# Prefetching DFT matrices, gating later loads and spreading row preparation in a fused S4 convolution and GLU MLP kernel

## The chip, the cores and the metric

The kernel runs on one core of a Trainium2 chip. The metric is the device time of one execution in microseconds (us), taken as the median of several runs; lower is better. The profiler's record of one execution has a *span*, which is about 2 us shorter than the device time of that execution (469.3 against 471.06 for the kernel before).

Engines are named as in the profile: PE is TensorE (matmuls), DVE is VectorE, ACT is ScalarE, POOL is GpSimd, and SP is SyncE, which here issues the DMA transfers. PEclk is the clock granted to TensorE, where 1.00 is full speed.

## The reference

The input `u` is [1, 2048, 640] in bf16. Cut to what matters:

```python
def _A_ref(u, A_re, A_im, B_re, B_im, C_re, C_im, log_dt, Dskip):
    ...                                             # K [640, 2048]: sums of complex exponentials
    Kf = rfft2(pad(K))[None]                        # zero-padded to 4096
    Uf = rfft2(pad(u.transpose(0, 2, 1)))
    y = irfft2(Uf * Kf)[..., :L]                    # long convolution by FFT
    return y.transpose(0, 2, 1) + u * Dskip

def _B_ref(x, w_gate, w_up, w_down):                # 640 -> 1728 -> 640
    return (sigmoid(x @ w_gate) * (x @ w_up)) @ w_down

x = A_u
h = x + _A_ref(_layernorm(x), ...)
h2 = h + _B_ref(_layernorm(h), ...)                 # the output
```

## The kernel before

The Fourier transforms are matmuls with constant DFT matrices. The 640 channels go in two halves of 320 columns (`HALVES`). After preparation (tables, first layer norm, spectrum of the input) three parts follow, and the change touches all three.

**1. Spectrum product, `kspec`.** There are 17 frequency groups q, taken in the order 16, 0, 1, ..., 15. Each needs a DFT matrix `mk` of 320 KB from DRAM. The pool `mkp` holds three of them.

```python
def front(qp):                                   # a pair of q
    W3 = mkp.tile(..., name="W3g");  sy.dma_start(W3..., cd["W3"]...)
    for qi, q in enumerate(qs):
        mk = mkp.tile([P, 2, 5, 128], BF16, name="mk")
        sy.dma_start(mk[:]..., cd["M"][q])                       # 320 KB
        ps = ps2.tile([P, 2, 512], F32, name="ps_xk", tag="p2")
        for ri in range(2):
            for j in range(5):                                   # 10 matmuls of 320 columns
                nc.tensor.matmul(ps[:, ri, 0:w], lhsT=mk[:, ri, j, :], rhs=kv[:, j, :], ...)
        nc.scalar.copy(xk[:, qi, :, :], ps[:, :, 0:w])
    ...                                          # DVE: products t1, t2 of xk with the input's spectrum xu
def back(qs, prods, W3):
    ...                                          # up to 8 matmuls into ps_g for each q
    nc.scalar.copy(stg[0][...], ps[:, :, 0:w])                   # g_stg
    if q % 2 == 1:
        sy.dma_start(d2[hf]..., stg[0][:])                       # to DRAM
```

**2. Hand-over.** The result `d2` comes back from DRAM as `g2` with rows on other partitions. For four tiles of 128 rows ("rows" below means such a tile), the skip term `us` and the last transform step are summed in PSUM, DVE adds the residual `h`, and layer norm and transposes follow. Only then can the first gate matmul run.

```python
def tail_loads(rc):                              # rc: row block of 4 tiles of 128 rows
    nc.sync.dma_start(h[:, 4*rc:4*rc+4, :], xv[:, 4*rc:4*rc+4, :])
    ...                                          # g2 of both halves, one DMA each
    return g2, [skip(h, 4*rc+i, sd) for i in range(4)]           # us: two DVE steps for each row

def prep(rc, loaded):
    is2(pso_p, "ml_po", rc, loaded)              # matmuls of us and g2, DVE: h += PSUM
    for r in range(r0, r0 + 4): ln_stats(st, mv, h, r)
    ln_coef(...)
    ...                                          # DVE: ln2 rows; PE: 20 transposes; DVE/ACT: copies to lnT
prep(0, first)
Wg, Wu, Wd = Wts()                               # 16 DMAs for gate, up, down weights
nxt = tail_loads(1)
```

**3. MLP.** Four row blocks of 512 rows. The hidden size 1728 makes 13 tiles of 128 and a tail of 64.

```python
FT = [(128 * i, 128) for i in range(13)] + [(1664, 64)]
for rc in range(4):
    for ft, (f0, fw) in enumerate(FT):
        for (ps, W) in ((pg, Wg), (pu, Wu)):
            for dc in range(5): nc.tensor.matmul(ps[0:fw, :], lhsT=W[:, dc, f0:f0+fw], rhs=lnT..., ...)  # 512 columns
        nc.scalar.activation(sg, pg, AF.Sigmoid);  nc.vector.tensor_tensor(hm, pu, sg, ALU.mult)
        if rc < 3 and ft == 4:
            prep(rc + 1, nxt)                    # the whole preparation of the next block, at once
            if rc < 2: nxt = tail_loads(rc + 2)
    ...                                          # down projection: 4 rows x 14 tiles x (512 + 128 columns)
```

## Time and profile before

The time before is 468.78 us (median of three runs, 464.31 to 470.15).

The span falls into stages whose limits differ. I cut it at the first `ps_xk` matmul of the second channel half, the end of its last `g_stg` copy, and the first gate or up matmul.

| stage of the kernel before | from – to, us | length, us | what limits it |
|---|---|---|---|
| preparation and first half | 0 – 179.6 | 179.6 | not changed |
| spectrum product, second half | 179.6 – 224.3 | 44.8 | waits for `mk` |
| hand-over | 224.3 – 248.1 | 23.7 | store, load of g2, sums, layer norm |
| MLP | 248.1 – 469.3 | 221.2 | TensorE |

These are the windows of the kernel before: the two middle stages, then the first two of the four row blocks. Columns: stretch and its length; then for each engine busy us (instructions); then granted clock, DMA busy share, GB/s.

```profile
core 0: us, PE busy (x) PEld busy (x) DVE busy (x) ACT busy (x) POOL busy (x), PEclk, DMA share, GB/s
179.60:224.30 44.70, 32.06 (x236) 19.21 (x236) 23.48 (x45) 21.64 (x33) 0.00 (x0) 0.96 0.92 295
224.30:248.10 23.80, 9.86 (x47) 5.39 (x48) 11.91 (x32) 1.21 (x3) 1.04 (x1) 0.58 0.97 338
248.10:305.60 57.50, 53.43 (x290) 26.18 (x293) 26.69 (x56) 10.81 (x17) 1.13 (x1) 0.94 0.09 30
305.60:363.00 57.40, 54.09 (x292) 26.56 (x296) 23.91 (x47) 9.53 (x16) 1.23 (x1) 0.94 0.03 12
```

In the first line TensorE works 32 of 44.7 us and the DMA engines are busy 92% of the time: this looks like a stage bound by bytes. In the second line the clock is 0.58. In the row blocks TensorE is busy nearly all the time, but each loses 3 to 4 us (the third, 56.0 us long, loses 2).

This is the chain of work that ended last in the kernel before, for the first two stages. Columns: start, duration, and what it was; "issue" is time in which the engine waited for nothing that the profile shows, and L446 is a line of the kernel (the numbers differ between kernels).

```profile
181.11 5.48 DMA mk<-s4c_M
186.59 0.04 issue
186.63 2.32 PE ps_xk L446 x10
...
224.36 3.10 DMA d_1_59<-g_stg
```

A `mk` line is a transfer from issue to landing; TensorE is idle in only a part of it. Three more such pieces stand in the chain, at 191.89, 204.32 and 214.67. After the last store the view goes on through Wd loads (down weights, not needed before the first down projection) and a g2 load of 8.20 us. That part misleads: `g_1_2622` in it is the g2 of the *second* block, which the first gate matmul doesn't need. The g2 load on which the hand-over hangs is `g_1_2468`, issued at 227.52 with Wd loads before and after it in the queue. The DMA view gives its time from issue to landing (size of one, then us):

```profile
g_1_2468<-d_1_59 SPq DMA_DIRECT2D x1, 640.0 KB, 6.2
```

This is what TensorE waits for in the kernel before, in the second half's stages and, after the dots, in the MLP. Columns: the waiting line and what it waited for; us in total, times, longest.

```profile
PE ps_xk L446 <- DMA mk<-s4c_M: 10.0, 5, 2.9
PE ps_y L505 <- DMA g_1_2468<-d_1_59: 7.4, 1, 7.4
...
PE ml_pt L641 <- DVE ln_2759 L637: 2.6, 1, 2.6
PE ml_pt L641 <- DVE ln_3191 L637: 2.2, 1, 2.2
```

Ten microseconds of waits for matrices are the largest single item. The transposes (`ml_pt`) in the MLP wait for DVE's layer-norm rows, because the whole preparation of a block is done in one bunch.

### The profile page before, as it was taken

The numbers are of one execution on the slowest core, as the hardware profiler recorded it, in microseconds if no ns is written. First come the engines' busy times: TensorE is split into PE (matmuls) and PEld (weight loads), VectorE is DVE, ScalarE is ACT, GpSimd is POOL, SyncE is SP. The second block draws the span as 40 slices with busy tenths as digits, with TensorE's granted clock in tenths as the row PEclk, the third lists the DMA queues.
The fourth block names the chain that finished last, engine by engine and source line by source line (L and its number), as shares of the span: only waits on it lengthen the run. The fifth ranks groups of instructions, "written<-read, shape, count | busy, mean of one in ns | idle before, by whom it ended". The sixth has DMA issues, their size and how long they took to land.

```text
span 469.3 us, 6215 instructions
## 1 busy us (share of the span) xinstructions
PE 353.4 (75%) x2412; PEld 188.2 (40%) x2435; DVE 276.6 (59%) x506; ACT 189.4 (40%) x323; POOL 9.9 (2%) x16
## 2 busy tenths in 40 slices
PE   1113643589997387876249799997999989999996
PEld 1001211276654174443125444544444444444443
DVE  4989899979999913554085843238322373322312
ACT  5989987466775363455003032020320203103210
POOL 0010100000000000000000000001000000000000
PEclk9999855569999679899569979999799999999999
DMA  8601654623997506799892300010000100010001
GB/s 242 243 1 56 219 202 128 181 68 87 284 303 246 162 1 239 242 315 299 287 377 94 113 0 1 0 57 1 1 0 1 56 1 0 1 55 2 0 16 42
DMA packets 47725, 54.23 MB, mean 116 GB/s; under 512 B 7056, under 2 KB 39888, under 8 KB 47696
## 3 DMA queue, kind: packets, MB, share of 16 engines
q1 hardware_dynamic: 47696, 53.84, 35.7%
q8 instruction: 19, 0.31, 0.3%
q14 instruction: 10, 0.08, 0.1%
HBM read 40.72 MB, written 13.11 MB: 115 GB/s over the span
## 4 chain that ended last, share of the span: by engine, by line
PE 38%; DVE 35%; issue 14%; DMA 9%; ACT 2%; POOL 1%; SPq 1%; POOLq 0%; DVEq 0%
PE ml_pg L656 10%; PE ml_po L670 9%; PE ml_pu L656 9%; DMA mk<-s4c_M 4%; PE pk L401 4%; DVE tabA L332 4%; DVE tS L330 4%; PE ps_xk L446 3%; DVE ln_st L250 3%; DVE tabB L347 2%; DVE tS L346 2%; DVE tabA L334 2%; DVE tabA L333 2%; DMA g_1_2622<-d_1_59 2%; PE ps_kv L412 1%
## 5 line engine op out<-in xcount | busy, mean ns | idle before, releaser
L659 DVE TENSOR_TENSOR ml_hm<-ml_pu,ml_sg 128x512 bf16<-128x512 f32 (+1 forms) x56 | 38.7, 691 | 79.2 <-PE ml_pu L656 69.8
L658 ACT ACTIVATE ml_sg<-ml_pg 128x512 bf16<-128x512 f32 (+1 forms) x56 | 33.4, 597 | 121.2 <-PE ml_pg L656 119.6
L656 PE MATMUL ml_pg<-lnT,Wg 128*128 128x512 bf16 (+1 forms) x272 | 71.1, 392 | 0.5 <-issue 0.2
L656 PE MATMUL ml_pu<-lnT,Wu 128*128 128x512 bf16 (+1 forms) x275 | 68.8, 379 | 0.3 <-issue 0.2
L670 PE MATMUL ml_po<-Wd,ml_hm 128*128 128x512 bf16 (+3 forms) x438 | 64.8, 298 | 0.6 <-issue 0.2
L446 PE MATMUL ps_xk<-kv,mk 128*128 128x320 bf16 x340 | 50.9, 303 | 14.1 <-DMA mk<-s4c_M 10.6
L670 PEld LDWEIGHTS <-ml_hm 128*128 128x128 bf16 x448 | 33.3, 98 | 31.8 <-issue 9.0
L446 PEld LDWEIGHTS <-mk 128*128 128x128 bf16 x340 | 32.8, 98 | 31.6 <-DMA mk<-s4c_M 13.7
L656 PEld LDWEIGHTS <-Wg 128*128 128x128 bf16 (+1 forms) x280 | 28.0, 102 | 35.3 <-issue 6.5
L656 PEld LDWEIGHTS <-Wu 128*128 128x128 bf16 (+1 forms) x280 | 27.6, 99 | 31.9
L672 DVE TENSOR_TENSOR ml_out<-ml_po,h 128x640 bf16<-128x640 f32 x16 | 13.2, 825 | 43.1 <-PE ml_po L670 43.1
L447 ACT CAST xk<-ps_xk 128x640 bf16<-128x640 f32 x34 | 23.5, 692 | 33.2 <-PE ps_xk L446 31.8
L642 ACT COPY lnT<-ml_pt 128x512 bf16<-128x512 bf16 x8 | 4.7, 586 | 62.6 <-PE ml_pt L641 62.6
L478 ACT CAST g_stg<-ps_g 128x640 bf16<-128x640 f32 x32 | 21.1, 697 | 8.8 <-PE ps_g L474 8.0
L361 PEld LDWEIGHTS <-c_F_102 128*128 128x128 bf16 x64 | 8.0, 125 | 41.1 <-issue 37.5
L401 PE MATMUL pk<-tabB,tabA 128*128 128x84 bf16 x320 | 19.2, 230 | 6.5 <-DVE tabA L333 4.6
L401 PEld LDWEIGHTS <-tabA 128*128 128x128 bf16 x320 | 17.0, 116 | 10.7 <-issue 10.0
L509 DVE TENSOR_TENSOR h<-ps_y,h 128x640 bf16<-128x640 f32 x16 | 12.8, 818 | 13.2 <-PE ps_y L505 12.0
L403 ACT CAST kts<-pk 128x420 bf16<-128x420 f32 x32 | 15.4, 511 | 12.1 <-PE pk L401 11.7
L332 DVE TENSOR_TENSOR tabA<-tabA 128x2240 bf16<-128x2240 bf16 (+2 forms) x16 | 18.9, 1194 | 0.0
L381 PEld LDWEIGHTS <-W2g 128*64 128x64 bf16 x136 | 8.3, 132 | 25.9 <-DMA W2g<-s4c_W 9.6
L330 DVE TENSOR_TENSOR tS<-tabA 128x2240 bf16<-128x2240 bf16 (+2 forms) x16 | 18.4, 1194 | 0.0
(335 smaller groups left out, 471.9 us busy)
## 6 DMA issues: line engine op xcount, KB each, us to landing
mk<-s4c_M SPq DMA_DIRECT2D x34, 320.0 KB, 4.5
d1u<-s_stg SPq DMA_DIRECT2D x16, 320.0 KB, 2.8
a2g<-d1u SPq DMA_DIRECT2D x16, 320.0 KB, 3.5
W3g<-s4c_W SPq DMA_DIRECT2D x16, 192.0 KB, 4.4
u<-in_A_u_dram SPq DMA_DIRECT2D x4, 640.0 KB, 6.3
d_0_58<-g_stg SPq DMA_DIRECT2D x8, 320.0 KB, 3.4
h<-in_A_u_dram SPq DMA_DIRECT2D x4, 640.0 KB, 8.4
d_1_59<-g_stg SPq DMA_DIRECT2D x8, 320.0 KB, 3.9
```

The source lines that it names most:

```text
L250: nc.vector.bn_stats(st[:, r, hh, :], src[:, r, 320 * hh:320 * hh + 320])
L330: V(t[:, ri], A[:, ri, :, s0:s1, :], bc(A[:, 1, :, b:b + 1, :], [P, G, n, 4]), ALU.mult)
L332: V(A[:, ri, :, d0:d1, :], A[:, ri, :, s0:s1, :], bc(A[:, 0, :, b:b + 1, :], [P, G, n, 4]), ALU.mult)
L401: nc.tensor.matmul(pk[:, i, :], lhsT=A[:, ri, g].rearrange("p e c -> p (e c)"), rhs=B[:, ri, :, 4 * g:4 * g + 4], start=(ri == 0), stop=(r ...
L403: nc.scalar.copy(kts[:, g0:g0 + 5, :], pk[:])
L446: nc.tensor.matmul(ps[:, ri, 0:w], lhsT=mk[:, ri, j, :], rhs=kv[:, j, :], start=(j == 0), stop=(j == 4))
L447: nc.scalar.copy(xk[:, qi, :, :], ps[:, :, 0:w])
L478: nc.scalar.copy(stg[0][:, 2 * (q % 2):2 * (q % 2) + 2, :], ps[:, :, 0:w])
L656: nc.tensor.matmul(ps[0:fw, :], lhsT=W[:, dc, f0:f0 + fw], rhs=rhs, start=(dc == 0), stop=(dc == 4))
L658: nc.scalar.activation(sg[0:fw, :], pg[0:fw, :], AF.Sigmoid)
L659: nc.vector.tensor_tensor(hm[0:fw, ft, :], pu[0:fw, :], sg[0:fw, :], ALU.mult)
L670: nc.tensor.matmul(po[:, c0:c0 + w], lhsT=hm[0:fw, ft, 128 * lr:128 * lr + 128], rhs=Wd[0:fw, ft, c0:c0 + w], start=(ft == 0), stop=(ft == ...
```

## The change

The change has five parts:

- eight DFT matrices of the second half are loaded early, into the slot of a tile (`xu0`) that is dead by then;
- Wd and the rows `h` of later blocks are *gated*: their loads wait for a small POOL copy from the first rows' layer-norm coefficients, so that they don't compete with the loads the hand-over needs;
- for the first four rows the residual is summed on TensorE with an identity matmul, and the layer-norm statistics are read from PSUM;
- the 64-wide tails of gate and up are merged into one 128-wide matmul;
- the preparation of the next row block is a generator, advanced one step for each tile from ft 5 on, with the transposes at ft 12.

The skip rows `us` also move, from the loads into the row sums. Three smaller edits go along: each g2 load is split into two of 320 KB, the first rows' layer-norm coefficients are computed by pairs of rows, and ACT computes two of the first four layer-norm rows.

```diff
+    NPRE = 8
+    def prefetch(kx):
+        mb = kx.tile([P, NPRE, 2, 5, 128], BF16, name="mk_pre", tag="X")       # xu0 has tag "X" too
+        for i in range(NPRE):
+            sy.dma_start(mb[:, i]..., cd["M"][QORD[i]])
 ...
-                mk = mkp.tile([P, 2, 5, 128], BF16, name="mk")
-                sy.dma_start(mk[:]..., cd["M"][q])
+                if pre is not None and QPOS[q] < NPRE:
+                    mk = pre[:, QPOS[q]]
+                else:
+                    ...                                                        # as before
 ...
+    def is2_row(rc, i, g2, h, us, psp, tag, stats=None):
 ...
+            if stats is not None:
+                nc.tensor.matmul(ps[:, hf, 0:w], lhsT=ident[:], rhs=h[:, r, o:o + w], start=False, stop=False)
 ...
+        else:
+            stats(r, ps[:, :, 0:w])                                            # bn_stats from PSUM
+            nc.scalar.copy(hv, ps[:, :, 0:w])
 ...
     drain(s2)
+    pre = prefetch(kx)
     kv = kmm(1, ktp, kx, dict(T))
 ...
+    def tail_loads(rc, gate=None):
+        if gate is not None:
+            nc.gpsimd.tensor_copy(h[:, rs, 0:1], bc(gate, [P, 4, 1]))
 ...
+def load_d(nc, wp, ins, gate):
     Wd = wp.tile([P, 14, 640], BF16, name="Wd", tag="B")
+    nc.gpsimd.tensor_copy(Wd[:, :, 0:1], bc(gate, [P, 14, 1]))
 ...
+            if rc < 3 and ft >= 5:
+                if ft == 5: pr = prep(rc + 1, nxt)
+                drain(pr, 1)
+                if ft == 8 and rc < 2: nxt = tail_loads(rc + 2, gate)
+                if ft == 12: turn(rc + 1)                                      # the transposes
 ...
+        for dc in range(5):                                                    # both 64-wide tails
+            nc.tensor.matmul(pg[:], lhsT=Wl[:, dc]..., rhs=rhs, ...)
```

More of the change, by code (lines that the diff above doesn't have):

```diff
@@ L428, in kmm, with kspec @@
         return kv
-    def kspec(hf, kv, xu, kw2, mkp, dve_add):
+    NPRE = 8
+    def prefetch(kx):
+        mb = kx.tile([P, NPRE, 2, 5, 128], BF16, name="mk_pre", tag="X")
+        for i in range(NPRE):
+            sy.dma_start(mb[:, i].rearrange("p a b c -> p (a b c)"), cd["M"][QORD[i]])
+        return mb
+    def kspec(hf, kv, xu, kw2, mkp, dve_add, pre=None):
         o, w = HALVES[hf]
@@ L440, in front @@
             for qi, q in enumerate(qs):
-                mk = mkp.tile([P, 2, 5, 128], BF16, name="mk")
-                sy.dma_start(mk[:].rearrange("p a b c -> p (a b c)"), cd["M"][q])
+                if pre is not None and QPOS[q] < NPRE:
+                    mk = pre[:, QPOS[q]]
+                else:
+                    mk = mkp.tile([P, 2, 5, 128], BF16, name="mk")
+                    sy.dma_start(mk[:].rearrange("p a b c -> p (a b c)"), cd["M"][q])
                 ps = ps2.tile([P, 2, 512], F32, name="ps_xk", tag="p2")
@@ L496, in skip @@
         return us
-    def is2(rc, g2, h, us4, psp, tag):
-        for i in range(4):
-            r = 4 * rc + i
-            ps = psp.tile([P, 2, 512], F32, name="ps_y", tag=tag)
-            for hf, (o, w) in enumerate(HALVES):
-                nc.tensor.matmul(ps[:, hf, 0:w], lhsT=ident[:], rhs=us4[i][:, o:o + w], start=True, stop=False)
-                for qp in range(2):
-                    nc.tensor.matmul(ps[:, hf, 0:w], lhsT=W4[:, qp, :], rhs=g2[hf][:, qp, i, :], start=False, stop=(qp == 1 and r < 12))
-                if r >= 12:
-                    nc.tensor.matmul(ps[:, hf, 0:w], lhsT=sel[0:4, r - 12, :], rhs=kl[0:4, o:o + w], start=False, stop=True)
-            hv = h[:, r, :].rearrange("p (a b) -> p a b", a=2)
+    def is2_row(rc, i, g2, h, us, psp, tag, stats=None):
+        r = 4 * rc + i
+        ps = psp.tile([P, 2, 512], F32, name="ps_y", tag=tag)
+        for hf, (o, w) in enumerate(HALVES):
+            nc.tensor.matmul(ps[:, hf, 0:w], lhsT=ident[:], rhs=us[:, o:o + w], start=True, stop=False)
+            if stats is not None:
+                nc.tensor.matmul(ps[:, hf, 0:w], lhsT=ident[:], rhs=h[:, r, o:o + w], start=False, stop=False)
+            for qp in range(2):
+                nc.tensor.matmul(ps[:, hf, 0:w], lhsT=W4[:, qp, :], rhs=g2[hf][:, qp, i, :], start=False, stop=(qp == 1 and r < 12))
+            if r >= 12:
+                nc.tensor.matmul(ps[:, hf, 0:w], lhsT=sel[0:4, r - 12, :], rhs=kl[0:4, o:o + w], start=False, stop=True)
+        hv = h[:, r, :].rearrange("p (a b) -> p a b", a=2)
+        if stats is None:
             nc.vector.tensor_tensor(hv, ps[:, :, 0:w], hv, ALU.add)
+        else:
+            stats(r, ps[:, :, 0:w])
+            nc.scalar.copy(hv, ps[:, :, 0:w])
     cb_product()
@@ L537, in full_kernel @@
     kx = sc.pool("xu", bufs=1)
-    xu0 = kx.tile([P, 17, 2, HALVES[0][1]], BF16, name="xu0")
+    xu0 = kx.tile([P, 17, 2, HALVES[0][1]], BF16, name="xu0", tag="X")
     ktp = sc.pool("kts", bufs=2)
@@ L572, in full_kernel @@
     dsk = tl.tile([P, D], BF16, name="dsk")
-    def tail_loads(rc):
-        nc.sync.dma_start(h[:, 4 * rc:4 * rc + 4, :], xv[:, 4 * rc:4 * rc + 4, :])
+    def tail_loads(rc, gate=None):
+        rs = slice(4 * rc, 4 * rc + 4)
+        if gate is not None:
+            nc.gpsimd.tensor_copy(h[:, rs, 0:1], bc(gate, [P, 4, 1]))
+        nc.sync.dma_start(h[:, rs, :], xv[:, rs, :])
         g2 = []
@@ L579, in tail_loads, with row @@
             v = d2[hf].rearrange("k (c a r) d -> (k c) a r d", c=4, a=2)
-            sy.dma_start(t[:], v[:, :, 4 * rc:4 * rc + 4, :])
+            for i in (0, 2):
+                sy.dma_start(t[:, :, i:i + 2, :], v[:, :, 4 * rc + i:4 * rc + i + 2, :])
             g2.append(t)
-        return g2, [skip(h, 4 * rc + i, sd) for i in range(4)]
-    drain(kspec(1, kv, xu1, kw2, mkp, True))
+        return g2
+    def row(psp, tag, rc, i, g2, stats=None):
+        r = 4 * rc + i
+        us = sd.tile([P, D], BF16, name="us")
+        nc.vector.tensor_scalar(us[:], h[:, r, :], rstd[:, r:r + 1], nmr[:, r:r + 1], ALU.mult, ALU.add)
+        nc.vector.tensor_tensor(us[:], us[:], dsk[:], ALU.mult)
+        is2_row(rc, i, g2, h, us, psp, tag, stats)
+    drain(kspec(1, kv, xu1, kw2, mkp, True, pre))
     sy.dma_start(dsk[:], ins["A_Dskip"].rearrange("(o d) -> o d", o=1).to_broadcast((P, D)))
@@ L587, in full_kernel @@
     sc.close("mk", "kw2", "a2", "kts", "xu", "ps_2", "ps_k")
-    mlp(nc, sc, h, lambda: load_gu(nc, wp, ins) + (load_d(nc, bp, ins),), ident, ov, ln_stats, ln_coef, first, tail_loads,
-        lambda psp, tag, rc, x: is2(rc, x[0], h, x[1], psp, tag))
+    mlp(nc, sc, h, lambda: load_gu(nc, wp, ins), lambda gate: load_d(nc, bp, ins, gate), ident, ov, ln_stats, ln_coef, first, tail_loads, row)
     sc.close("sd", "g2", "tl", "weights", "tabb", "consts", "dram")
+FT = 13
 def load_gu(nc, wp, ins):
-    Wg = wp.tile([P, 5, 1728], BF16, name="Wg")
-    Wu = wp.tile([P, 5, 1728], BF16, name="Wu")
+    Wg = wp.tile([P, 5, 1664], BF16, name="Wg")
+    Wu = wp.tile([P, 5, 1664], BF16, name="Wu")
+    Wl = wp.tile([P, 5, 2, 64], BF16, name="Wl")
     gv = ins["B_w_gate"].rearrange("(c p) f -> p c f", p=P)
     uv = ins["B_w_up"].rearrange("(c p) f -> p c f", p=P)
-    for f0 in range(0, 1728, 432):
-        nc.sync.dma_start(Wg[:, :, f0:f0 + 432], gv[:, :, f0:f0 + 432])
-        nc.sync.dma_start(Wu[:, :, f0:f0 + 432], uv[:, :, f0:f0 + 432])
-    return Wg, Wu
-def load_d(nc, wp, ins):
+    for f0 in range(0, 1664, 416):
+        nc.sync.dma_start(Wg[:, :, f0:f0 + 416], gv[:, :, f0:f0 + 416])
+        nc.sync.dma_start(Wu[:, :, f0:f0 + 416], uv[:, :, f0:f0 + 416])
+    nc.sync.dma_start(Wl[:, :, 0, :], gv[:, :, 1664:1728])
+    nc.sync.dma_start(Wl[:, :, 1, :], uv[:, :, 1664:1728])
+    return Wg, Wu, Wl
+def load_d(nc, wp, ins, gate):
     Wd = wp.tile([P, 14, 640], BF16, name="Wd", tag="B")
+    nc.gpsimd.tensor_copy(Wd[:, :, 0:1], bc(gate, [P, 14, 1]))
     for c in range(0, 13, 2):
@@ L608, in load_d, with mlp @@
         nc.sync.dma_start(Wd[:, c:c + n, :], ins["B_w_down"][128 * c:128 * (c + n), :].rearrange("(c p) f -> p c f", p=P))
-    nc.sync.dma_start(Wd[0:64, 13, :], ins["B_w_down"][1664:1728, :])
+    nc.sync.dma_start(Wd[64:128, 13, :], ins["B_w_down"][1664:1728, :])
     return Wd
-def mlp(nc, sc, h, Wts, ident, ov, ln_stats, ln_coef, first, tail_loads, is2):
+def mlp(nc, sc, h, gu, down, ident, ov, ln_stats, ln_coef, first, tail_loads, row):
     big = sc.pool("ml_big", bufs=1)
@@ L626, in mlp, with stats_first, turn @@
     nmr = big.tile([P, 16], F32, name="ln2_nmr")
+    def stats_first(r, src):
+        for hh in range(2):
+            nc.vector.bn_stats(st[:, r, hh, :], src[:, hh, :])
+        nc.vector.bn_aggr(mv[:, r, :], st[:, r, :, :].rearrange("p a b -> p (a b)"))
+        if r % 2:
+            ln_coef(mv, rstd, nmr, slice(r - 1, r + 1))
     def prep(rc, loaded):
         r0 = 4 * rc
-        is2(pso_p, "ml_po", rc, loaded)
-        for r in range(r0, r0 + 4):
-            ln_stats(st, mv, h, r)
-        ln_coef(mv, rstd, nmr, slice(r0, r0 + 4))
         ln2 = lnp.tile([P, 4, 640], BF16, name="ln2")
         for i in range(4):
-            r = r0 + i
-            nc.vector.tensor_scalar(ln2[:, i, :], h[:, r, :], rstd[:, r:r + 1], nmr[:, r:r + 1], ALU.mult, ALU.add)
+            row(pso_p, "ml_po", rc, i, loaded, stats_first if rc == 0 else None)
+            if rc:
+                ln_stats(st, mv, h, r0 + i)
+                yield
+        if rc:
+            ln_coef(mv, rstd, nmr, slice(r0, r0 + 4))
+        for i in range(4):
+            r = r0 + i
+            if rc == 0 and i % 2:
+                nc.scalar.activation(ln2[:, i, :], h[:, r, :], AF.Identity, scale=rstd[:, r:r + 1], bias=nmr[:, r:r + 1])
+            else:
+                nc.vector.tensor_scalar(ln2[:, i, :], h[:, r, :], rstd[:, r:r + 1], nmr[:, r:r + 1], ALU.mult, ALU.add)
+            if rc and i % 2:
+                yield
+        lns[rc] = ln2
+    lns = {}
+    def turn(rc):
+        ln2 = lns[rc]
         for dc in range(5):
@@ L641, in prep @@
                 nc.tensor.transpose(pt[:, i, :], ln2[:, i, 128 * dc:128 * dc + 128], ident[:])
-            (nc.scalar.copy if dc % 2 else nc.vector.tensor_copy)(lnT[:, dc, r0:r0 + 4, :], pt[:])
-    prep(0, first)
-    Wg, Wu, Wd = Wts()
-    nxt = tail_loads(1)
-    FT = [(128 * i, 128) for i in range(13)] + [(1664, 64)]
+            (nc.scalar.copy if dc % 2 else nc.vector.tensor_copy)(lnT[:, dc, 4 * rc:4 * rc + 4, :], pt[:])
+    drain(prep(0, first))
+    turn(0)
+    Wg, Wu, Wl = gu()
+    gate = nmr[:, 3:4]
@@ L648, in mlp, with up @@
+    Wd = down(gate)
+    nxt = tail_loads(1, gate)
     for rc in range(4):
+        pr = None
         hm = hmp.tile([P, 14, 512], BF16, name="ml_hm")
-        for ft, (f0, fw) in enumerate(FT):
+        def up(ps, W, f0):
+            for dc in range(5):
+                rhs = lnT[:, dc, 4 * rc:4 * rc + 4, :].rearrange("p a b -> p (a b)")
+                nc.tensor.matmul(ps[:], lhsT=W[:, dc, f0:f0 + 128], rhs=rhs, start=(dc == 0), stop=(dc == 4))
+        for ft in range(FT):
             pg = psg_p.tile([P, 512], F32, name="ml_pg", tag="ml_pg")
@@ L652, in mlp @@
             pu = psu_p.tile([P, 512], F32, name="ml_pu")
-            for (ps, W) in ((pg, Wg), (pu, Wu)):
-                for dc in range(5):
-                    rhs = lnT[:, dc, 4 * rc:4 * rc + 4, :].rearrange("p a b -> p (a b)")
-                    nc.tensor.matmul(ps[0:fw, :], lhsT=W[:, dc, f0:f0 + fw], rhs=rhs, start=(dc == 0), stop=(dc == 4))
+            up(pg, Wg, 128 * ft)
+            up(pu, Wu, 128 * ft)
             sg = tmp.tile([P, 512], BF16, name="ml_sg")
-            nc.scalar.activation(sg[0:fw, :], pg[0:fw, :], AF.Sigmoid)
@@ L659, in mlp @@
-            nc.vector.tensor_tensor(hm[0:fw, ft, :], pu[0:fw, :], sg[0:fw, :], ALU.mult)
-            if rc < 3 and ft == 4:
-                prep(rc + 1, nxt)
-                if rc < 2:
-                    nxt = tail_loads(rc + 2)
+            nc.scalar.activation(sg[:], pg[:], AF.Sigmoid)
+            nc.vector.tensor_tensor(hm[:, ft, :], pu[:], sg[:], ALU.mult)
+            if rc < 3 and ft >= 5:
+                if ft == 5:
+                    pr = prep(rc + 1, nxt)
+                drain(pr, 1)
+                if ft == 8 and rc < 2:
+                    nxt = tail_loads(rc + 2, gate)
+                if ft == 12:
+                    turn(rc + 1)
@@ new lines, in mlp @@
+        pg = psg_p.tile([P, 512], F32, name="ml_pg", tag="ml_pg")
+        for dc in range(5):
+            rhs = lnT[:, dc, 4 * rc:4 * rc + 4, :].rearrange("p a b -> p (a b)")
+            nc.tensor.matmul(pg[:], lhsT=Wl[:, dc].rearrange("p a b -> p (a b)"), rhs=rhs, start=(dc == 0), stop=(dc == 4))
+        sg = tmp.tile([P, 512], BF16, name="ml_sg")
+        nc.scalar.activation(sg[64:128, :], pg[0:64, :], AF.Sigmoid)
+        nc.vector.tensor_tensor(hm[64:128, FT, :], pg[64:128, :], sg[64:128, :], ALU.mult)
@@ L667, in mlp @@
             po = pso_p.tile([P, 640], F32, name="ml_po")
-            for ft, (f0, fw) in enumerate(FT):
+            for ft in range(14):
+                k0 = 64 if ft == FT else 0
                 for (c0, w) in ((0, 512), (512, 128)):
-                    nc.tensor.matmul(po[:, c0:c0 + w], lhsT=hm[0:fw, ft, 128 * lr:128 * lr + 128], rhs=Wd[0:fw, ft, c0:c0 + w],
+                    nc.tensor.matmul(po[:, c0:c0 + w], lhsT=hm[k0:128, ft, 128 * lr:128 * lr + 128], rhs=Wd[k0:128, ft, c0:c0 + w],
                                      start=(ft == 0), stop=(ft == 13))
```

## The prediction

> **What bounds it now.** Three stages (windows, chain of waits, timeline):
>
> 1. 179–225 us, last half of the spectrum product. DMA is 90% busy at 290 GB/s, PE only 33 of 46 us. The chain waits four times for a DFT matrix (mk): 5.48, 4.89, 5.09, 4.87 us. Between waits a pair of q takes 3.66 us on PE (199.13 to 202.79), so 17 q need about 31 us.
> 2. 224–248 us, hand-over: last store of d2 3.1 us, then the g2 load, beside the Wd loads, arrives at 233.8; sums, LN, transposes until the first gate matmul at 248.08. 23.7 us, DMA at 99%, granted clock 0.5 to 0.7.
> 3. 248–466 us, MLP, PE bound. Row blocks with preparation take 57 us, the last, without, 47. PE waits for the LN rows (2.6, 2.2, 0.9 us) and for copies of the transposes; the clock drops to 0.83 in 260–274 and 0.86 in 327–351.
>
> **What changes, costed.**
>
> - *Prefetch.* xu0's slot is free at 159.5 us, and DMA is idle in 165–179. Eight matrices (2.6 MB, 8 us at the 345 GB/s of 225–248) land before 179; three more were already early. Only 6 of 17 stay in the busy stage. The weights and rows ahead of them, about 6.4 MB, 19 us, land about when the tenth q is done: little waiting. End of stage 224 → about 215 (−9).
> - *Gated loads.* Wd and the later h wait for the first rows' LN coefficients, so the critical g2 load, now in halves, competes with little: 6.2 us → about 3.5 (−2.5).
> - *First rows summed on TensorE, stats from PSUM.* Adds 8 identity matmuls of 320 columns; takes the DVE add (0.82 us a row) off the chain, and the next block's skip rows (0.44 + 0.49 us each), which DVE now runs between the LN steps. But the third and fourth row reuse two PSUM buffers, at half clock (0.27 us per 320 columns, 0.136 warm): −2 net. First gate matmul about 234–235 instead of 248.
> - *64-wide tails merged.* 5 fewer 512-column matmuls per block: 4 × 5 × 0.216 = −4.3.
> - *Preparation spread.* Needed PE work per block is 24 × 0.136 plus transposes, about 5 us, against 10 lost now: −5 for each of three blocks, partly by the clock not falling. DVE needs 3.5 us a tile with a row against 3.0 on PE, for four tiles; two PSUM buffers absorb this.
> - *Given back.* h of the second block now queues behind 2.2 MB of Wd, issued around 232; it lands near 243, when in-order DVE wants it after the third tile: +1.5.
>
> Sum: −9 −2.5 −2 −4.3 −15 +1.5 ≈ −31, all on the chain, because each stage starts when the former ends. Predicted 438 us, 431 to 449.
>
> The Trainium skill, "TensorE: Matmul & The Clock Gate" (Part 1: The HAM clock gate), says that an idle PE falls to half clock and needs sustained work to recover; this trace agrees (0.50 in 225–235, 1.00 in 410–450). So removing waits also removes slow matmuls.
>
> **What would show it.** mk waits under 4 us in total; last d2 store about 10 us earlier; first gate matmul 234–236; row blocks of about 51, 51, 51, 46 us; clock near 1.00 from 250 on; PE waits before transposes under 2 us in the MLP.
>
> **What would make it wrong.** Weights loaded ahead delay the last six mk or the d2 stores; TensorE sums at half clock cost more than the DVE adds saved; DVE, waiting for the gated h, holds back the gate products; Wd late for the first down projection; the clock falling without waits.
>
> Chances: faster 0.97, same 0.02, slower 0.01.

## The result

| kernel | median us | range | runs |
|---|---|---|---|
| before | 469.46 | 464.31 – 470.76 | 4 |
| after | 444.79 | 442.80 – 445.57 | 4 |

(One run of before was added to the three quoted above.) The ratio is 0.9491, with a 95% interval of 0.9423 to 0.9558. Ratios in this document are the mean time of one kernel's fast runs over that of the other's of the same rounds, so they are not quite the ratio of the medians quoted. A step of 0.01 in such a ratio is 4.7 us. Of the runs of the kernel before, two of seven in the first call and three of seven in the second were slow; the ratios leave these out, the medians of before quoted below don't.

The changed kernel's windows, cut at the same events and with the same columns:

```profile
178.60:220.80 42.20, 33.18 (x236) 19.56 (x236) 23.55 (x45) 21.59 (x33) 0.00 (x0) 0.91 0.93 280
220.80:238.70 17.90, 10.60 (x49) 5.92 (x49) 6.38 (x20) 5.21 (x8) 2.08 (x6) 0.60 0.54 157
238.70:291.10 52.40, 52.40 (x298) 25.96 (x297) 29.03 (x64) 11.39 (x18) 1.24 (x1) 0.95 0.32 108
291.10:340.80 49.70, 49.70 (x292) 24.95 (x291) 24.22 (x47) 9.52 (x16) 1.01 (x1) 1.00 0.04 14
```

In the row blocks, TensorE's busy time now equals the length: 52.40 of 52.40, 49.70 of 49.70 (and 52.60 of 52.60 in the third). In the hand-over the DMA share fell from 0.97 to 0.54. The first line is the surprise: the stage that lost eight of its loads is only 2.5 us shorter, at the same DMA share, and at a lower clock.

| stage | before | after | difference | predicted |
|---|---|---|---|---|
| start of the second half | 179.56 | 178.62 | −0.9 | – |
| spectrum product | 44.8 | 42.2 | −2.6 | −9 |
| hand-over | 23.7 | 17.9 | −5.9 | −4.5 |
| MLP | 221.2 | 203.5 | −17.7 | −17.8 |

(The predicted −4.5 is −2.5 − 2, and −17.8 is −4.3 − 15 + 1.5, all from the text of the prediction. The differences add up to −27.1, and the medians differ by 24.7 only: the profiled run of before, with 471.06 us, was slower than its median.)

This is the chain after, over the same time:

```profile
176.79 5.87 DMA h<-in_A_u_dram
...
183.59 0.80 DVE us L609 x2
184.39 0.74 DVE t_2067 L462
...
196.20 5.82 DMA mk<-s4c_M
202.01 0.05 issue
202.06 2.33 PE ps_xk L457 x10
...
209.99 0.37 SPq L491
...
210.96 4.34 DMA mk<-s4c_M
...
223.31 3.44 DMA g_1_2462<-d_1_59
```

Two of the `mk` pieces are left. The Wd loads are gone from the hand-over, and the first block's g2, now in halves, takes 3.44 us (its first half) instead of 6.2. And a piece stands in front that the chain before doesn't show: the load of the rows `h`, then skip rows (`us`) on DVE, ahead of the product `t_2067`, which TensorE needs. It is new in the chain, but not new on DVE: in the kernel before, DVE did the same in the same order, later still (skip rows from 184.23, product from 185.75). There TensorE waited for a matrix until 186.63 and then had its ten matmuls to do, so the delay on DVE was hidden.

What TensorE waits for in the changed kernel, in the same stages:

```profile
PE ps_xk L457 <- DMA mk<-s4c_M: 4.7, 2, 2.4
PE ps_y L517 <- DMA g_1_2462<-d_1_59: 2.6, 1, 2.6
PE ps_g L485 <- DVE t_2067 L465: 2.2, 1, 2.2
...
```

The waits for matrices fell from 10.0 to 4.7 us, and 2.2 us of waiting for `t_2067` came into the open. From 248 us on the same view is empty for the changed kernel: in the MLP TensorE waits for nothing.

### The profile page after: what moved, and what is told of

It reads as the page before. It is cut to its first block, busy times and chain, and to the rows that moved or that the text cites. A ratio compares the mean times of both kernels' runs of the same rounds, so it can differ in the third digit from the quotient of the medians.

```text
span 442.2 us, 6255 instructions
## 1 busy us (share of the span) xinstructions
PE 345.8 (78%) x2423; PEld 185.1 (42%) x2423; DVE 274.0 (62%) x502; ACT 193.7 (44%) x329; POOL 10.8 (2%) x21
## 4 chain that ended last, share of the span: by engine, by line
PE 56%; DVE 33%; DMA 6%; ACT 2%; issue 1%; POOL 1%; SPq 1%; DVEq 0%; ACTq 0%; POOLq 0%
PE ml_po L745 14%; PE ml_pg L712 13%; PE ml_pu L712 13%; DVE tabA L332 4%; PE pk L401 4%; DVE tS L330 4%; PE ps_xk L457 3%; DVE tabB L347 3%; DVE tS L346 2%; DMA mk<-s4c_M 2%; DVE tabA L334 2%; PE ps_y L517 2%; DVE tabA L333 2%; DVE tabB L349 2%; DVE tabB L348 1%
## 5 line engine op out<-in xcount | busy, mean ns | idle before, releaser
L720 ACT ACTIVATE ml_sg<-ml_pg 128x512 bf16<-128x512 f32 x52 | 31.1, 597 | 135.0 <-PE ml_pg L712 131.8
L721 DVE TENSOR_TENSOR ml_hm<-ml_pu,ml_sg 128x512 bf16<-128x512 f32 x52 | 35.7, 686 | 49.9 <-PE ml_pu L712 49.9
L712 PE MATMUL ml_pu<-lnT,Wu 128*128 128x512 bf16 x260 | 65.9, 384 | 0.0
L745 PE MATMUL ml_po<-Wd,ml_hm 128*128 128x512 bf16 x448 | 65.9, 299 | 0.0
L712 PE MATMUL ml_pg<-lnT,Wg 128*128 128x512 bf16 x260 | 65.9, 385 | 0.0
L457 PE MATMUL ps_xk<-kv,mk 128*128 128x320 bf16 x260 | 39.8, 306 | 8.0 <-DMA mk<-s4c_M 5.8
L747 DVE TENSOR_TENSOR ml_out<-ml_po,h 128x640 bf16<-128x640 f32 x16 | 13.2, 825 | 44.7 <-PE ml_po L745 44.7
L712 PEld LDWEIGHTS <-Wu 128*128 128x128 bf16 x260 | 25.6, 99 | 30.9 <-issue 0.8
L712 PEld LDWEIGHTS <-Wg 128*128 128x128 bf16 x260 | 25.2, 99 | 29.8 <-issue 2.4
L458 ACT CAST xk<-ps_xk 128x640 bf16<-128x640 f32 x34 | 23.5, 692 | 27.1 <-PE ps_xk L457 25.7
L403 ACT CAST kts<-pk 128x420 bf16<-128x420 f32 x32 | 15.3, 511 | 11.4 <-PE pk L401 11.1
L485 PEld LDWEIGHTS <-W3g 64*128 64x128 bf16 x198 | 9.4, 98 | 17.6 <-issue 13.4
L346 DVE TENSOR_TENSOR tS<-tabB,tabMB 128x1280 bf16<-128x1280 bf16 (+2 forms) x18 | 16.1, 895 | 0.2
```

What stands on the lines that cost most here:

```text
L346: V(t, X[:, :, src, :], mm, ALU.mult)
L403: nc.scalar.copy(kts[:, g0:g0 + 5, :], pk[:])
L712: nc.tensor.matmul(ps[:], lhsT=W[:, dc, f0:f0 + 128], rhs=rhs, start=(dc == 0), stop=(dc == 4))
L720: nc.scalar.activation(sg[:], pg[:], AF.Sigmoid)
L721: nc.vector.tensor_tensor(hm[:, ft, :], pu[:], sg[:], ALU.mult)
L745: nc.tensor.matmul(po[:, c0:c0 + w], lhsT=hm[k0:128, ft, 128 * lr:128 * lr + 128], rhs=Wd[k0:128, ft, c0:c0 + w], start=(ft == 0), stop=(f ...
```

## The experiments

Two questions were open. Why did the stage shorten by 2.6 us and not by 9? And is each of the other terms what the prediction said? Each run is compared with the kernel before on the same chip and in the same rounds. The medians of before were 468.5, 469.93 and 467.69 us in the three calls.

For the stage there were three theories:

- **Slots.** With three slots for the last matrices, a load can only be issued when an earlier matrix has been multiplied. More early matrices remove the waits.
- **Order on DVE.** The skip rows of the first block, which wait for `h`, stand in DVE's in-order queue in front of products that are ready.
- **Bytes.** The stage is bound by the DMA engines (share 0.93). Then moving a few loads does nothing.

### no_prefetch: the change without its prefetch

```diff
-    pre = prefetch(kx)
+    pre = None
```

> The changed kernel without the prefetch alone. In the changed kernel the spectrum stage (first ps_xk to last g_stg copy) took 42.2 us against 44.8 before, though waits of 9 us were to go. Theory A (new waits ate the gain: vector engine in order behind the h load, last six matrices behind the weights): the stage goes back to 44 to 46 us, so the run is 2 to 4 us slower than the changed kernel, near 448. Theory B (the prefetch gave its 9 us, another part of the change took 6 back in this stage): the run is 8 to 10 us slower, near 454.

Measured: 446.9 us, ratio 0.9561 [0.9499, 0.9623]. The stage took 43.4 us, the hand-over 19.4. TensorE waited five times for `mk`, 7.6 us in all. The prefetch is worth 3 to 4 us in this kernel (0.9561 against 0.9491, or 0.9483 in the repetition below; the intervals overlap). That is the first theory's total, but only 1.2 to 1.5 us of it are in the stage; as much is in the hand-over.

### only_prefetch: the kernel before with the prefetch alone

```diff
+    pre = prefetch(kx)                            # with the branch in front(), and xu0 in the slot "X"
-    drain(kspec(1, kv, xu1, kw2, mkp, True))
+    drain(kspec(1, kv, xu1, kw2, mkp, True, pre))
```

> The kernel before with the prefetch alone. Theory A: the stage shortens by 2 to 4 us, total 465 to 467 against 469. Theory B: by 8 to 10 us, total near 460. If the weights that now go out early only shift traffic to the hand-over, part may be lost there, or gained there, because Wd then starts earlier.

Measured: 460.46 us, ratio 0.9862 [0.9797, 0.9928]. Alone on the kernel before, the prefetch brings 6.5 us by the ratio (8 by the medians). The two profiled runs differ by more, 11.4 us: 3.6 in the stage (41.2 us), nothing in the hand-over (23.8) and 7.3 in the first row block, which takes 50.2 us instead of 57.5. So the stage fits the first theory, and the total is close to what the second one expected, for another reason. In its hand-over TensorE executed 65 instructions, against 47 before; 48 of them are matmuls of row sums, against 26. A block needs 24, so the rows of the *second* block arrived early and were summed while TensorE would have been idle. The parts of the change are not additive: the gates forbid this early work.

### skip_late: skip rows behind the second pair's products

The first rows' `us` read a copy of `rstd` that DVE writes only after the second pair's products; that is a false dependence and leaves the results unchanged.

```diff
+                if late is not None and qp == 1:
+                    nc.vector.scalar_tensor_tensor(late[:], t1[:, 0, 0, 0:16], 0.0, rstd[:], ALU.mult, ALU.add)
-        nc.vector.tensor_scalar(us[:], h[:, r, :], rstd[...], ...)
+        nc.vector.tensor_scalar(us[:], h[:, r, :], (rs2 if rc == 0 else rstd)[...], ...)
```

> The changed kernel with the skip rows of the first block made to wait for the second pair of spectrum products, so that the vector engine no longer stands in order behind the h load (landed at 182.7) while the first products are ready at 182. Theory A: the wait of TensorE for t1 of the first pair (2.2 us, and some half clock after it) goes; 1.5 to 3 us faster than the changed kernel, if the last matrices do not absorb it. Rival (stage bound by bytes: 12 MB at 280 to 300 GB/s): no change, within 1 us, because the waits for mk grow by as much.

Measured: 442.67 us, ratio 0.9464 [0.94, 0.9527]. DVE's timeline shows the delay and its removal. Columns: start, us, engine, line, operation, tiles and shapes, count, and in brackets the idle time before with what ended it. First the kernel before, then the changed kernel, then this one:

```profile
184.23 0.80 DVE L494 TENSOR_SCALAR us<-h,rstd,nmr 128x640 bf16<-128x640 bf16 x2 [4.46 <-DMA h<-in_A_u_dram]
...
185.75 0.82 DVE L451 TENSOR_TENSOR t_2062<-xu_1049,xk 128x1280 bf16<-128x1280 bf16 x1
```

```profile
182.79 0.80 DVE L608 TENSOR_SCALAR us<-h,rstd,nmr 128x640 bf16<-128x640 bf16 x2 [3.96 <-DMA h<-in_A_u_dram]
183.51 0.89 DVE L609 TENSOR_TENSOR us<-us,dsk 128x640 bf16<-128x640 bf16 x2
184.31 0.82 DVE L462 TENSOR_TENSOR t_2067<-xu_1049,xk 128x1280 bf16<-128x1280 bf16 x1
```

```profile
183.16 0.83 DVE L462 TENSOR_TENSOR t<-xu,xk 128x1280 bf16<-128x1280 bf16 x1 [3.43 <-ACT xk L458]
```

In the changed kernel DVE idles 3.96 us until `h` lands, does four skip steps, and starts the product at 184.31. Here the product starts 3.6 us after the stage's start (at 179.53) instead of 5.7 us after it. The Trainium skill, "TensorE: Matmul & The Clock Gate" (Part 1, Architectural detail), says that ACT and DVE are strictly first in, first out; this trace agrees, since nothing overtook the waiting skip step for 3.96 us. The stage shortened by about 1 us (41.0 against 42.2 and 41.9), less than the 1.5 to 3 expected: part of the gain was taken back by a longer wait for `mk` (5.1 us in all, the longest 3.0). In total the gain is about 1 us by the ratios, and the intervals overlap, so the effect on the stage is seen but its worth in time is small and not resolved by itself.

### mk13: thirteen early matrices instead of eleven

With eight prefetched and three slots in the pool, eleven matrices were already early. Two more now go into slots of another pool that is idle at that time.

```diff
+                    if a2p is not None and QPOS[q] < NPRE + 2:
+                        mk = a2p.tile([P, 2, 5, 128], BF16, name="mk_a2", tag="a2g")
+                    else:
+                        mk = mkp.tile([P, 2, 5, 128], BF16, name="mk")
```

> The changed kernel with two more matrices loaded early, into the idle slots of the a2 pool: 13 of 17 are there before the stage, and a slot frees 5 products before it is needed instead of 3. Theory A: the two waits for mk (2.3 and 2.4 us, plus about 1.3 us of half clock after them) go, 3 to 5 us faster than the changed kernel. Rival (bytes): within 1 us, DMA share of the stage stays at 0.93 and TensorE waits elsewhere, for W3 or the d2 stores.

Measured: 440.01 us, ratio 0.9415 [0.9355, 0.9475]: 3.2 to 3.6 us better than the changed kernel by the ratios, as expected, though the intervals still overlap. This is the window of its stage (columns as before):

```profile
179.05:217.00 37.95, 30.91 (x236) 19.22 (x236) 23.46 (x45) 21.47 (x33) 0.00 (x0) 1.00 0.98 293
```

And this is its TensorE timeline at the only wait for `mk` that is left:

```profile
205.71 1.53 PE L460 MATMUL ps_xk<-kv,mk 128*128 128x320 bf16 x10 [1.43 <-DMA mk<-s4c_M]
```

The stage is 4.2 us shorter than that of the changed kernel (3.9 against its repetition below), and the clock in it is 1.00 instead of 0.91. The waits for `mk` fell from 4.7 to 1.4 us. Slower matmuls are most of the rest: TensorE was busy for 30.91 us instead of 33.18 with the same 236 matmuls. After its 1.43 us wait the ten matmuls took 1.53 us, while after waits of 2.31 and 2.40 us in the changed kernel they took 2.33 and 1.99. So *Slots* is right. *Bytes* falls: the stage moved 11.1 MB (293 GB/s times 37.95 us) against 11.8 (280 times 42.2), 6% fewer bytes for a stage 10% shorter. The last but one kernel below is clearer still: it moved the same 11.8 MB in 36.9 us.

The arithmetic of the slots, from the chain: the matrix issued at 196.20 was issued as soon as an earlier one had been multiplied (196.10), and landed 5.82 us later. Two matrices in hand keep TensorE busy for one pair, 3.66 us. The difference is 2.2 us; the wait was 2.31. By this arithmetic three slots are one too few for a load of 5 to 6 us. It also gives the wait that is left in mk13: issued at 199.96, landed 5.71 us later, wanted after 4.3. The second wait of the changed kernel had another cause: SP is in order, too, and the load issued at 210.96 stood behind a store (`L491`) that waited for ACT's copy.

### tails64: the 64-wide tails as two matmul groups again

```diff
-        for dc in range(5):                                     # one group with Wl[:, dc] of 128
+        for gi, ps in enumerate((pg, pu)):
+            for dc in range(5):
+                nc.tensor.matmul(ps[0:64, :], lhsT=Wl[:, dc, gi, :], rhs=rhs, ...)
```

> The changed kernel with the gate and up tails of 64 columns apart again, 5 more matmuls of 512 columns in each of 4 row blocks. If the term was sized right: 4 x 5 x 0.216 = 4.3 us slower than the changed kernel, 1.1 us in each block. Rival: at the end of a block TensorE waits for the last gate product anyway; then less than 1 us shows.

Measured: 451.41 us, ratio 0.9652 [0.9572, 0.9732]. The MLP took 209.0 us against 203.5, so the merge is worth 5.5 us there, somewhat more than the 4.3 of the matmuls alone. The total moved by more, 7.5 to 8 us by the ratios; its profiled run also has a stage of 43.9 us, which the edit doesn't touch, so I count the 5.5 only.

### bunched: the preparation at once after tile 4, as before

```diff
-            if rc < 3 and ft >= 5:
-                ...                                             # one step for each tile
+            if rc < 3 and ft == 4:
+                drain(prep(rc + 1, nxt))
+                turn(rc + 1)
```

> The changed kernel with the preparation of a row block run in one piece after the fifth tile and transposed at once, as before, not spread. If the spreading is what gave 5 to 6 us in each of three blocks: blocks of 55 to 57 us instead of 51 to 52, with waits of TensorE for the LN rows of 2 us and a fallen clock; 12 to 17 us slower than the changed kernel. Rival (the gain came mostly from the skip rows leaving the vector engine's queue and from the early loads): under 6 us slower.

Measured: 459.49 us, ratio 0.9841 [0.9749, 0.9933]: the largest single part of the change, 14.4 us in the MLP (217.9 against 203.5). The waits of TensorE in the MLP are back, where the changed kernel has none:

```profile
PE ml_pt L696 <- DVE ln L684: 5.2, 3, 2.5
PE ps_y L513 <- DVE us L609: 2.0, 1, 2.0
```

With 1.9 us for copies of the transposes these waits are 9 us in all; the row blocks took 59.7, 55.0 and 54.4 us. By the windows TensorE was idle for about 11 us in these three blocks and busy for 3.4 us longer than in the changed kernel, so the waits and slower matmuls are two parts of one cost. The 2.0 us of waiting for `us` are not part of the kernel before, which computed these rows at the loads; so this run somewhat overstates what spreading alone brings.

### ungated: Wd and the later rows without gates

```diff
-    nc.gpsimd.tensor_copy(Wd[:, :, 0:1], bc(gate, [P, 14, 1]))
-    nxt = tail_loads(1, gate)
+    nxt = tail_loads(1)                                         # tail_loads(rc + 2) likewise
```

> The changed kernel without the two gates: Wd and the later h may load as soon as the queue comes to them. If the gate protects the critical g2 load: the hand-over (last g_stg copy to the first gate or up matmul) grows from 17.9 to 20 to 21 us, TensorE's wait for g2 from 2.6 to 5 to 6, total 2 to 3 us slower. Rival (after the prefetch the queue is nearly empty by then, so the gate protects nothing): under 1 us; or faster, because h arrives earlier.

Measured: 441.49 us, ratio 0.9457 [0.9378, 0.9535]. The hand-over became 1.3 to 1.5 us longer (19.4), as the gates' purpose demands. The time was not lost in the g2 load, though. These are the two halves in the changed kernel, then here:

```profile
g_1_2462<-d_1_59 SPq DMA_DIRECT2D x2, 320.0 KB, 3.6
```

```profile
g<-d SPq DMA_DIRECT2D x2, 320.0 KB, 3.6
```

They are equally fast, although Wd loads issued before them were still under way here. What grew is the store in front of them, the last one of `d2`: 3.83 us against 2.45 (3.03 in the repetition below). But the first row block shrank from 52.4 to 47.3 us, because the second block's rows were summed in the hand-over again (67 TensorE instructions in it, against 49). The gates as a whole cost rather than bring time; by the ratios it is 1.2 to 1.6 us, and the intervals overlap.

### dve_sums: the first rows' residual added on DVE

```diff
-            row(pso_p, "ml_po", rc, i, loaded, stats_first if rc == 0 else None)
+            row(pso_p, "ml_po", rc, i, loaded)
+            ln_stats(st, mv, h, r0 + i)
```

> The changed kernel with the first rows as before: h added by the vector engine, statistics read from h in SBUF, coefficients still by pairs of rows. If TensorE sums shorten the hand-over as predicted (2 us): 2 us slower. Rival: at half clock the 8 added identity matmuls (0.27 us each) cost as much as the vector adds (0.82 us a row) saved; then within 1 us, or faster.

Measured: 443.17 us, ratio 0.9478 [0.9411, 0.9545]. The hand-over is 1.0 to 1.2 us longer (19.1): without the TensorE sums the transposes wait 5.3 us for the layer-norm rows, against 2.8. In the total no difference is seen (0.9478 against 0.9483 and 0.9491). The first row block is 51.4 us long here and 52.4 in the changed kernel, but it is 51.3 in mk13 and 51.5 in skip_late, whose edits don't touch it either; so where the microsecond went is not shown.

### after_again: the changed kernel once more, five rounds

There is no edit; the kernel is the changed one.

> The changed kernel once more, so that the parts are compared with it in the same rounds and its stages have a second trace. 444 to 446 us, ratio 0.945 to 0.953; stage 42 to 43, hand-over 18, MLP 203 to 204.

Measured: 443.14 us (442.39 to 446.9, six runs), ratio 0.9483 [0.9448, 0.9519]; stage 41.9, hand-over 18.1, MLP 203.3. It is the yardstick for the next three, which ran in the same rounds.

### h_free: only the gate of the second block's rows removed

```diff
-    nxt = tail_loads(1, gate)
+    nxt = tail_loads(1)                                         # Wd stays gated
```

> The changed kernel with Wd still gated but h of the second row block free to load early. Without both gates the hand-over grew by 1.5 us and the first row block shrank by 5, because TensorE summed rows of the second block while it waited for the first block's LN. If the gate on h is what costs: first block 47 to 48 us instead of 52, hand-over 18 to 19, total 3 to 5 us under the changed kernel. Rival (the first block gained from Wd being there early, not from h): no change from the changed kernel.

Measured: 441.44 us, ratio 0.9437 [0.9402, 0.9471]. That is 1.7 us under after_again (2.2 by the ratios), less than the 3 to 5 expected; the intervals still overlap a little. The first row block took 48.8 us. The profiled run happened to be the slowest of the six (445.11), with a clock of 0.86 and a length of 44.7 us in the stage, so its stages are used with reserve.

### best: mk13, skip_late and h_free together

> Three repairs together on the changed kernel: 13 matrices early, the first skip rows behind the second pair of products, h of the second block free. If the stage waits and the h gate are independent: 4.5 (mk) + 1 (skip) + 4 (h) = 8 to 10 us under the changed kernel, 435 to 437. If they share their gain: 438 to 440.

The edit is those three diffs together. Measured: 434.98 us (434.15 to 435.08, five runs), ratio 0.9292 [0.927, 0.9315]: 8.2 us under the changed kernel in the same rounds, and 7.1% under before. Its windows of stage, hand-over and first row block:

```profile
178.80:215.70 36.90, 30.90 (x236) 19.29 (x236) 25.01 (x50) 21.48 (x33) 0.00 (x0) 1.00 1.03 320
215.70:234.30 18.60, 12.79 (x67) 7.45 (x67) 10.01 (x28) 5.19 (x7) 1.85 (x5) 0.63 0.54 154
234.30:281.80 47.50, 47.50 (x281) 23.41 (x278) 24.61 (x52) 11.39 (x18) 1.01 (x1) 1.00 0.32 105
```

The stage is 5 us shorter than in after_again, the first row block almost 5 us; the hand-over gives back half a microsecond while doing 18 more matmuls. The waits for `mk` are down to 0.7 us. The DMA share of 1.03 at 320 GB/s shows that the 0.93 and 280 GB/s of the changed kernel were no ceiling.

### best_warm: best, with filler matmuls to raise the clock in the hand-over

The clock in the hand-over is 0.5 to 0.75 in every kernel. Seven matmuls without use before the first rows' sums, and four before the transposes, were to keep TensorE busy.

```diff
+    def warm(n, src):
+        pu = psu_p.tile([P, 512], F32, name="ml_pu")
+        for i in range(n):
+            nc.tensor.matmul(pu[:], lhsT=ident[:], rhs=src, start=True, stop=True)
+    warm(7, h[:, 0, 0:512])
     drain(prep(0, first))
+    warm(4, lns[0][:, 0, 0:512])
     turn(0)
```

> The version with three repairs, with 7 matmuls of 512 columns that nobody reads put before the first sums and 4 more before the transposes, so that TensorE does not stand idle in the hand-over. If the half clock there (0.5 to 0.7) costs what it seems: rows 3 and 4 at 0.136 instead of 0.27 us per matmul, 2 to 4 us less. Rival (the filler runs at half clock itself, 3 us, and delays the sums, or the clock still comes too late): same or up to 2 us slower.

Measured: 434.91 us, ratio 0.9292 [0.9268, 0.9316]: nothing gained. TensorE's timeline in the hand-over of this kernel:

```profile
222.08 0.70 PE L522 MATMUL ps_y<-g,c_W 128*128 128x320 bf16 x4 [0.17 <-DMA g<-d]
224.45 0.31 PE L518 MATMUL ps_y<-us,c_ident 128*128 128x320 bf16 x1 [1.66 <-ACT h L530]
224.58 0.44 PE L520 MATMUL ps_y<-h,c_ident 128*128 128x320 bf16 x1
224.81 0.74 PE L522 MATMUL ps_y<-g,c_W 128*128 128x320 bf16 x2
```

The seven fillers, at 216.14, took 3.14 us, and they did raise the clock (four matmuls in 0.70 us at 222.08). Then TensorE waited 1.66 us for ACT to empty a PSUM buffer, and the rows behind it ran at half clock again (two matmuls in 0.74 us). The hand-over was about 1.3 us shorter, the first row block 0.6 us longer, and the total is unchanged. The two traces of the changed kernel point the same way: with a clock of 0.60 and 0.75 in the hand-over it took 17.9 and 18.1 us, so the clock did not set its length.

## Why the prediction was right, and where it was not

**Total: right.** Predicted were 438 us and a range of 431 to 449; measured, 444.79. The result is 7 us slower than the central value, and that has one main source.

**The step that failed: "End of stage 224 → about 215 (−9)".** The mechanism, waits for matrices, was right, and the waits did halve. The size was wrong: the end of the stage moved to 220.8, and the stage shortened by 2.6 us (2.9 in the repetition). "Little waiting" for the last six matrices was the false assumption. I counted bytes: would the data have arrived by the time it is wanted? I should have counted slots: when can the load be *issued*? A load of 5.82 us, issued when two matrices are left, which last 3.66 us, makes a wait of 2.2 us. mk13 shows it: two more early matrices made the stage 4.2 us shorter. A second, smaller part was not foreseen at all: the skip rows stood in front of ready products on DVE already in the kernel before, and the early matrices took away the wait for `mk` that hid this (2.2 us of waiting on TensorE, and 1.8 in only_prefetch, where nothing but the prefetch was added; about 1 us of the stage in skip_late). And each of the two waits for `mk` cost another 0.5 to 0.8 us in that run through the clock (1.99 and 2.33 us for ten matmuls, against 1.53). In the sum of the first profile: 5.3 us less waiting for `mk`, 2.2 more for `t_2067`, and TensorE busy for 1.1 us longer (33.18 against 32.06), which leaves about 2 of the 2.6. With both repaired, and one gate removed, the stage took 36.9 us; the forecast of −9 would have been 35.8.

The Trainium skill, "DMA: Bandwidth & Descriptors" (Rules for kernel authors), advises to issue the DMA early and wait on its semaphore late. The runs agree (−6.5 us by the prefetch alone on the kernel before), with the addition that "early" has to hold for the last matrix of a rotating buffer, too.

**First gate matmul "about 234–235": missed, 238.7.** The shift is the stage's; the hand-over itself shrank by 5.9 us against 4.5 predicted. From the experiments, with one profile each, gates give 1.3 to 1.5 of it, TensorE sums 1.0 to 1.2, and the prefetch 1.3 to 1.5; the remainder of about 2 us is not assigned by a run of its own. The halved g2 loads and the second block's skip rows, which no longer run between the layer-norm steps, are candidates.

**Gated loads "−2.5", given back "+1.5": the sign of the sum was probably wrong.** The critical g2 load did become as short as predicted ("6.2 us → about 3.5"; measured 3.44), but not by the gates: in ungated its first half took 3.45 us. Undivided and without gates, in only_prefetch, it took 4.68; so the prefetch and the halving seem to share this gain, while the gates shortened the last store. The skill's page "DMA: Bandwidth & Descriptors" (Queues, rings and completion order) says that descriptors are consumed in ring order on each DMA engine; the trace agrees: in the kernel before, the 22 loads and stores issued from 217 to 240 us landed in the order of their issue. What is given back is 3.6 to 5 us in the first row block (52.4 against 48.8 in h_free and 47.3 in ungated), not 1.5: without the gate on `h`, rows of the second block are summed while TensorE would otherwise wait. Removing both gates was faster by 1.2 to 1.6 us, removing that of `h` alone by 1.7; both are likely, neither is beyond the intervals.

**TensorE sums "−2 net":** about −1 in the hand-over, and none seen in the total.

**Tails "−4.3":** 5.5 us in the MLP. **Spread "−15":** 14.4 us in the MLP, but 7.3, 5.3 and 1.9 in the three blocks and not 5 in each. The row blocks were 52.4, 49.7 and 52.6 us against "51, 51, 51", and no wait of TensorE is left there. These two terms are the result; the reading that the MLP is bound by TensorE, so that matmuls removed and waits removed count in full, held. That the MLP came out at −17.7 against −17.8 is partly luck: 5.5 and 14.4 less 3.6 to 5 given back would be 15 to 16.

**The clock.** The prediction leaned on the skill's page "TensorE: Matmul & The Clock Gate" (Part 1: The HAM clock gate): a TensorE that idles falls to half clock. The trace agrees as far as waits and half clock go together: ten matmuls took 2.33 us after a wait of 2.31 us and 1.53 after none, and from 291 us on, without waits, the clock is 1.00. But not every wait of this length did it. In the changed kernel, then in the kernel before:

```profile
202.06 2.33 PE L457 MATMUL ps_xk<-kv,mk 128*128 128x320 bf16 x10 [2.31 <-DMA mk<-s4c_M]
```

```profile
219.59 1.53 PE L446 MATMUL ps_xk<-kv,mk 128*128 128x320 bf16 x10 [2.93 <-DMA mk<-s4c_M]
```

**Not settled.** Which of two waits of equal length halves the clock; why `h` (640 KB) takes 5.9 us at a time when few loads stand in front of it; why the clock of the stage differs between runs of one kernel (0.91 and 0.96 for the changed kernel, 0.86 in h_free). How much of the 5.82 us of a late matrix is due to the weight loads queued ahead of it was argued but not measured by itself.

## What to carry to other kernels

Size a prefetch by slots and issue times: the load that decides is the one that has to wait for a slot, and it costs its landing time less the work still in hand, and sometimes slower matmuls after the wait. When you remove a wait, look at what it hid: here, work on an in-order engine that stood in front of ready work. When you withhold loads to protect a critical one, look for idle time that the withheld data would have filled. Spreading preparation over a loop bound by TensorE pays twice, by the waits and by the clock.

## What the Trainium skill lacked or had wrong

- "TensorE: Matmul & The Clock Gate" gives an idle window of about 3.4 us for the fall to half clock and warns of idle gaps longer than that. Here shorter waits sometimes sufficed: after 2.31 and 2.40 us (changed kernel) and 2.84 us (before) ten matmuls took 2.33, 1.99 and 2.32 us; but after 2.40 and 2.93 us in the kernel before they took 1.53. In best_warm even 1.66 us was enough, shortly after a stretch at half clock. The page does say that the window is free-running, which may be why the outcomes differ, but it has no rule for waits shorter than the window.
- "DMA: Bandwidth & Descriptors" has no figure for how long a load takes to land in a queue that is already busy, which is what decides the number of slots. Here a load of 320 KB took 5.82 and 4.34 us in one stage (DMA share 0.93), and one of 640 KB took 5.87.
- The same page's rule to issue early and wait late says nothing of rotating buffers: with three slots of 320 KB a load could be issued no earlier than 3.66 us before it was wanted, and the wait was 2.31 us.
